# Attention followed by a squared-ReLU feed-forward: loads of later batches held back, batch 1's inputs loaded ahead of the weights, its turns moved into batch 0

## The chip, the cores and the metric

One core of a Trainium2 chip. The metric is device time in microseconds (us), lower is better. All runs quoted here were classed fast.

Names used for the engines in the profile: PE is TensorE (matrix multiplication; PEld its weight loads), ACT is ScalarE, DVE is VectorE, POOL is GpSimd, SP is the sync engine, which only issues transfers here.

Words used below: a **turn** is a transpose; on TensorE it is three matmuls against the identity matrix, and another engine copies its result out. **Idle matmuls** work on zeros, only to keep TensorE busy. The **granted clock** is the share of full speed that TensorE was given (1.00 is full); in a window it is a mean. A load **lands** when the last of its sixteen semaphore increments has come.

## The reference

```python
B, Hq, Hkv, S, D = 8, 16, 4, 384, 64                      # grouped-query attention, f32 inputs
scores = (q @ k.T) / sqrt(D)                              # k and v repeated 4 times over the heads
attn   = softmax(scores)                                  # per head, over 384 keys
x      = (attn @ v).transpose(0, 2, 1, 3).reshape(3072, 1024)
h      = maximum(x @ w_in, 0)                             # w_in 1024 x 2048
out    = (h * h) @ w_out                                  # w_out 2048 x 1024
```

## The kernel before

Eight batches (b0 to b7) of eight head pairs each. Pair n belongs to batch n // 8. The feed-forward network (FFN) of batch b runs on TensorE in between the attention of later batches. All inputs are f32 in HBM; loads issued by GpSimd cast them to bf16 on the way. Only b0 comes in as f32, over the queues of SP and ACT.

A recorder derives the semaphore waits; every engine runs its instructions in the order in which they are added. So an instruction that waits for data stops everything behind it on its engine. The order in which loads are added to GpSimd is also the order in which they get the DMA engines.

The loads and the start of b0 (cuts marked `...`):

```python
    cast_q(0)                       # f32 -> bf16 on GpSimd, one head pair
    load_w_in(0)                    # GpSimd queue, 0.52 MB of bf16 each
    cast_q(1)
    ...                             # v of b0
    for c in range(2, NPB):
        cast_q(c)
        load_w_in(c - 1)
    load_w_in(7)
    load_k(1); load_q(1); load_v(1) # one line each in the kernel
    for i in range(2):
        load_w_out(i)               # 2.10 MB of bf16 each
    load_k(2); load_q(2); load_v(2)
```

`prepare(b)`, called in pair 4 of the batch before, duplicates k of batch b on VectorE, turns k and q by DMA transposes on the sync queue, and then lets the loads of batch b + 1 go:

```python
    def prepare(b):
        dup_all_k(b)                # VectorE: waits for the load of k
        ...                         # dma_start_transpose of kT, then of qT in two parts
        if b + 1 < B:
            load_k(b + 1, [last])   # last = the second qT transpose
            load_q(b + 1, [last])
            load_v(b + 1, [last])
```

The main loop from pair 8 on. `fill(ns)` puts so much FFN work there; `put_x` turns a pair's attention output into x transposed (xT), by DMA. FFN(1) may start after pair 16, and needs xT of pair 15:

```python
    PER_PAIR = {1: 2700.0, **{b: 5100.0 for b in range(2, B + 1)}}
    ...
    for n in range(NPB, NP + 1):
        per = PER_PAIR[n // NPB]
        if n < NP:
            scores_pair(n)
        fill(per * 0.4)
        if n > NPB:
            attend(n - 1, 0)
        fill(per * 0.2)
        if n > NPB:
            attend(n - 1, 1)
            put_x(n - 1)
        if n % NPB == 4 and n // NPB + 1 < B:
            prepare(n // NPB + 1)
        if n % NPB == 7 and n // NPB + 1 < B:
            prepare_v(n // NPB + 1)
        fill(per * 0.4)
        ready[0] = max(0, n // NPB - 1)
```

The softmax here doesn't subtract the row's maximum and nothing guards it: scores larger than these inputs give would overflow.

Of the kernel before, what the change touches and what calls it, by code (L numbers as in the profile page):

```python
# [106 lines left out]
def bass_gqa_attention__then__ffn_squared_relu_kernel(  # L107
# [8 lines left out]
    bf16 = mybir.dt.bfloat16  # L116
    f32 = mybir.dt.float32

    B, H, S, D = 8, 16, 384, 64
    HKV = 4  # L120
    NJ = S // 128
    FF = 2048
    F = H * D
    NPB = H // 2
# [5 lines left out]
    R = Recorder(nc)  # L130
# [95 lines left out]
    for i in range(2):  # L226
        R.add("gpsimd", lambda e, i=i: e.memset(v_aug[i][:, :, D:D + 1], 1.0), writes=[("v_one", i)])

    def cast_q(c):
        R.add("gpsimd", lambda g: g.tensor_copy(q_st[0][:, 2 * c:2 * c + 2, :], q_f[:, 2 * c:2 * c + 2, :]),  # L230
              reads=[("q_f", c)], writes=[("q_st", 0, c)])

    cast_q(0)
    load_w_in(0)
    cast_q(1)
    R.add("gpsimd", lambda g: g.tensor_copy(
        v_aug[0][:, :, 0:D], v_f.ap().rearrange("p g j d -> p (g j) d")),
        reads=["v_f"], writes=[("v_aug", 0)])
    for c in range(2, NPB):
        cast_q(c)  # L240
        load_w_in(c - 1)
    load_w_in(7)
    load_k(1)
    load_q(1)
    load_v(1)
    for i in range(2):
        load_w_out(i)
    load_k(2)
# [19 lines left out]


    slots = [0]  # L270
    RING, FREE = (4, 5), (0, 1, 2, 3)
    sc_bf = sc_ps.ap().bitcast(bf16)

    def turn_bank(banks):
        i = banks[slots[0] % len(banks)]
        slots[0] += 1
        if i == 5:
            return f_ps[1].ap().bitcast(bf16)[:, 0:S], ("f_ps", 1)
        return sc_bf[:, i, 0:S], ("sc", i)

    def turn_on_pe(src, src_keys, dst, dst_key, banks):
        ps, key = turn_bank(banks)

        def tr(pe):
            for t in range(NJ):
                m = pe.matmul(ps[:, t * 128:(t + 1) * 128], src[:, t * 128:(t + 1) * 128], ident[:],  # L286
                              is_transpose=True)
            return m

        R.add("tensor", tr, reads=[*src_keys, "ident"], writes=[key])  # L290
        R.add("vector", lambda e: e.tensor_copy(dst, ps), reads=[key], writes=[dst_key])  # L291

    def dup_k(b, g):
        src = (k_f if b == 0 else k_st[b % NKS])[:, g].unsqueeze(2).to_broadcast([128, NJ, 2, D])
        R.add("vector", lambda e: e.tensor_copy(k_dup[b % 2][:, g * NJ:(g + 1) * NJ], src),
              reads=[("k_f", g) if b == 0 else ("k_st", b % NKS)], writes=[("k_dup", b % 2, g)])

    def first_kT(g, b=0):
        if b == 0:
            dup_k(0, g)  # L300
        turn_on_pe(k_dup[b][:, g * NJ:(g + 1) * NJ].rearrange("p a x d -> p (a x d)"), [("k_dup", b, g)],
                   kT[b][:, g], ("kT", b, g), FREE if b else RING)

    def first_qT(c, b=0):
        turn_on_pe(q_st[b][:, 2 * c:2 * c + 2, :].rearrange("p h e -> p (h e)"), [("q_st", b, c)],
                   qT[b][:, c], ("qT", b, c), FREE if b else RING)

    def first_oT(c, banks=RING):
        turn_on_pe(o_sb[c % NO].ap().rearrange("p i s d -> p (i s d)"), [("o_sb", c % NO, x) for x in range(2)],
                   xT[0][:, c], ("xT", 0, c), banks)  # L310

    def dup_all_k(b):
        src = k_st[b % NKS].ap().rearrange("p g j d -> p (g j) d").unsqueeze(2)
        R.add("vector", lambda e: e.tensor_copy(
            k_dup[b % 2][:, :, :, :], src.to_broadcast([128, HKV * NJ, 2, D])),
            reads=[("k_st", b % NKS)], writes=[("k_dup", b % 2, g) for g in range(HKV)])

    def prepare(b):
        st = b % NST
        dup_all_k(b)  # L320
        R.add("sync", lambda e: e.dma_start_transpose(
            kT[b % 2].ap().rearrange("p g (j c) -> p (g j) c", j=NJ),
            k_dup[b % 2].ap().rearrange("p a x d -> p (a x d)")),
            reads=[("k_dup", b % 2, g) for g in range(HKV)],
            writes=[("kT", b % 2, g) for g in range(HKV)], dma=f"kt{b % 2}")
        for part in range(2):
            cs = range(4 * part, 4 * part + 4)
            last = R.add("sync", lambda e, cs=cs: e.dma_start_transpose(
                qT[b % 2][:, cs.start:cs.stop, :].rearrange("p h (t c) -> p (h t) c", t=NJ),
                q_st[st][:, 2 * cs.start:2 * cs.stop, :].rearrange("p h e -> p (h e)")),  # L330
                reads=[("q_st", st, c) for c in cs], writes=[("qT", b % 2, c) for c in cs],
                dma=f"qt{b % 2}_{part}")
        if b + 1 < B:
            load_k(b + 1, [last])
            load_q(b + 1, [last])
            load_v(b + 1, [last])

    def prepare_v(b):
        R.add("vector", lambda e: e.tensor_copy(
# [73 lines left out]

    def put_x(p):
        b, c = p // NPB, p % NPB
        R.add("sync", lambda e: e.dma_start_transpose(
            xT[b % NXT][:, c, :].rearrange("p (i c) -> p i c", i=NJ),
            o_sb[p % NO].ap().rearrange("p i s d -> p (i s d)")),
            reads=[("o_sb", p % NO, x) for x in range(2)], writes=[("xT", b % NXT, c)], dma=f"xt{p % 8}")
# [2 lines left out]
    tiles = [0]  # L422

    def up_step(b, c, k0, k1, u, r):
        def mm(pe):
            for kc in range(k0, k1):
                m = pe.matmul(f_ps[u][:, 0:S], w_in_sb[:, kc, c * 128:(c + 1) * 128],  # L427
                              xT[b % NXT][:, kc, :], start=(kc == 0), stop=(kc == NKC - 1))
            return m

        R.add("tensor", mm, reads=[("w_in", c * 128 // WC)] +
              [("xT", b % NXT, kc) for kc in range(k0, k1)], writes=[("f_ps", u)])
        if k1 == NKC:
            R.add("vector", lambda e: e.tensor_scalar_max(hr[r][:, :], f_ps[u][:, 0:S], 0.0),  # L434
                  reads=[("f_ps", u)], writes=[("hr", r)])
            R.add("scalar", lambda e: e.activation(h2T[b % 2][:, c, :], hr[r][:, :], AF.Square),  # L436
                  reads=[("hr", r)], writes=[("h2T", b % 2, c)])
        return (k1 - k0) * 165
# [22 lines left out]
    def feed_forward(b):  # L461
        first = 0
        if b == 0:
            for c, k in ((0, 0), (0, 2), (0, 4), (1, 0), (1, 2), (1, 4), (0, 6), (1, 6)):
                yield up_step(b, c, k, k + 2, c, c)
            tiles[0] += 2
            first = 2
        for c in range(first, NFC):
            for k in range(0, NKC, 4):
                yield up_step(b, c, k, k + 4, tiles[0] % 2, tiles[0] % NHR)  # L470
            tiles[0] += 1
        for jj in range(2):
            for i in range(NJ):
                for part in range(4):
                    yield down_step(b, i, jj, part, tiles[0] % 2)
                tiles[0] += 1
# [9 lines left out]

    ffn = all_feed_forward()
    credit = [0.0]
    PER_PAIR = {1: 2700.0, **{b: 5100.0 for b in range(2, B + 1)}}

    def fill(ns):
        credit[0] += ns
        while credit[0] > 0:
# [3 lines left out]
                return  # L497
            credit[0] -= t

    idle(13)  # L500
    first_kT(0)
    idle(2)
    first_qT(0)
    idle(3)
    for n in range(NPB):
        early = n in (5, 6)
        scores_unit(n, 0)
        if early:
            next(ffn)
        elif n < 2:  # L510
            idle(2 - n)
        if n >= 1:
            attend(n - 1, 0)
        scores_unit(n, 1)
        if n % 2 == 1 and n + 1 < NPB:
            first_kT((n + 1) // 2)
        if n + 1 < NPB:
            first_qT(n + 1)
        if n >= 1:
            attend(n - 1, 1)  # L520
        scores_unit(n, 2)
        idle(1)
        if n >= 2:
            first_oT(n - 2)
    next(ffn)
    attend(NPB - 1, 0, True)
    first_oT(NPB - 2, (4,))
    attend(NPB - 1, 1, True)
    for _ in range(3):
        next(ffn)  # L530
    idle_on_sc(2)
    first_oT(NPB - 1, (0,))
    idle_on_sc(3)
    fill(6000.0)
    dup_all_k(1)
    fill(1500.0)
    for g in range(HKV):
        first_kT(g, 1)
        fill(700.0)
    prepare_v(1)  # L540
    for c in range(NPB):
        first_qT(c, 1)
        fill(500.0)
    for n in range(NPB, NP + 1):
        per = PER_PAIR[n // NPB]
        if n < NP:
# [4 lines that stand above are left out]
        fill(per * 0.2)  # L551
        if n > NPB:
            attend(n - 1, 1)
            put_x(n - 1)
        if n % NPB == 4 and n // NPB + 1 < B:
            prepare(n // NPB + 1)
        if n % NPB == 7 and n // NPB + 1 < B:
# [3 lines that stand above are left out]
# [32 lines left out]
```

## Time and profile before

447.52 us, median of 3 runs (445.23 to 447.89). What matters, from the profile of one execution (span 445.5 us):

| | before |
|---|---|
| TensorE busy | 430.6 us, 97% |
| first scores of b0 | 6.5 us |
| first scores of b1 (pair 8) | 47.9 us |
| wait for xT of pair 15 | 5.4 us idle, then low clock |
| granted clock 85 to 90, 90 to 95 us | 0.79, 0.53 |
| last landing of w_in, w_out; of k, q, v of b2 | 32.1, 58.4; 59.5, 64.5, 67.1 us |

The page of the kernel before: its first line, the busy times, and the granted clock in 40 slices of 11 us each (9 is full speed).

```profile
span 445.5 us, 8213 instructions
...
PE 430.6 (97%) x3589; PEld 239.8 (54%) x3626; DVE 165.9 (37%) x357; ACT 199.5 (45%) x209; POOL 33.2 (7%) x48
...
PEclk9999999979999999999999999999999999999999
```

The waits of TensorE in the kernel before, the longest in total: who waited for whom, total us, how often, the longest.

```profile
PE f_ps L427 <- DMA xT<-o_sb: 5.4, 1, 5.4
PE f_ps L256 <- DVE warm L221: 1.1, 1, 1.1
PE po L398 <- ACT expT L360: 0.9, 3, 0.4
```

The chain of waits of the kernel before, around the end of pair 16: start, us, what.

```profile
83.27 0.80 PE f_ps L445 x3
84.07 6.76 DMA xT<-o_sb
90.82 0.05 issue
90.87 4.00 PE f_ps L427 x12
```

The same stretch in windows: start and end, length, then busy us of PE, PEld, DVE, ACT, POOL, and last the granted clock, the DMA share and GB/s.

```profile
80.00:85.00 5.00, 4.95 (x45) 2.57 (x45) 1.63 (x4) 2.37 (x2) 0.00 (x0) 1.00 1.16 130
85.00:90.00 5.00, 0.43 (x3) 0.04 (x1) 0.00 (x0) 1.81 (x1) 0.00 (x0) 0.79 1.49 180
90.00:95.00 5.00, 4.13 (x22) 2.12 (x23) 0.65 (x2) 0.52 (x1) 0.00 (x0) 0.53 0.13 39
```

And the transfers issued from 76 to 90 us: KB each, median us from issue to landing.

```profile
q_st<-in_q_dram POOLq DMA_DIRECT2D x1, 768.0 KB, 12.5
...
xT<-o_sb SPq DMA_TRANSPOSE x3, 6.8
```

Read together: TensorE is the limit nearly everywhere, and its one large idle stretch is a wait for a small transfer that shares the DMA engines with a load nobody needs yet. Over the whole trace such a transfer takes 2.4 us (median). The rules table of the Trainium skill's page "DMA: Bandwidth & Descriptors" (section "Rules for kernel authors") says that queues of different engines run on the same 16 DMA engines and interleave; the 6.8 us here, on the sync queue beside a GpSimd load, agree.

### The profile page before, as it was taken

The page shows a single profiled execution, that of the slowest core. Times are in us where ns is not written, and L with a number is a line of the kernel's source. Part 1 is how long each engine was busy: PE and PEld are TensorE (multiplying, and loading weights), DVE is VectorE, ACT ScalarE, POOL GpSimd, SP SyncE. Part 2 cuts the span into 40 slices and gives each one's busy share as a digit, 9 for nine tenths or more (in the row PEclk, how much of TensorE's full clock was granted, in tenths as well). Part 3 has the DMA queues.
Part 4 walks back from the last instruction along what each step waited for, and adds up shares of the span by engine and source line. Part 5 has one row for each costly group of instructions (what it writes and reads, how often), then busy time and mean ns, then how long its engine had stood idle before and what let it go on. Part 6 is the DMA issues. An engine that isn't in the chain of part 4 may idle for free.

```text
span 445.5 us, 8213 instructions
## 1 busy us (share of the span) xinstructions
PE 430.6 (97%) x3589; PEld 239.8 (54%) x3626; DVE 165.9 (37%) x357; ACT 199.5 (45%) x209; POOL 33.2 (7%) x48
## 2 busy tenths in 40 slices
PE   8989999689999999999999999999999999999997
PEld 4556555346545665456644565456655565545543
DVE  2646432224423442334423434234423344224411
ACT  4953655325533564336632565236633466203400
POOL 5920001000020001000020000100000000000000
PEclk9999999979999999999999999999999999999999
DMA  9999998920495108920399106951252200220011
GB/s 244 197 196 203 209 192 190 147 43 16 90 167 122 43 10 149 175 85 10 76 147 151 45 20 126 139 113 42 32 135 82 66 20 18 66 81 24 1 71 71
DMA packets 95939, 44.70 MB, mean 100 GB/s; under 512 B 74400, under 2 KB 89760, under 8 KB 95904
## 3 DMA queue, kind: packets, MB, share of 16 engines
q0 software_dynamic: 34288, 16.65, 30.0%
q1 hardware_dynamic: 59504, 25.96, 25.4%
q10 hardware_dynamic: 2112, 1.57, 1.1%
q8 instruction: 28, 0.46, 0.5%
q14 instruction: 7, 0.06, 0.0%
HBM read 35.65 MB, written 12.58 MB: 108 GB/s over the span
## 4 chain that ended last, share of the span: by engine, by line
PE 94%; DMA 2%; DVE 2%; ACT 1%; issue 1%
PE f_ps L427 38%; PE f_ps L445 37%; PE po L398 8%; PE sc_ps L370 7%; DMA xT<-o_sb 2%; PE sc_ps L354 1%; ACT expT L360 1%; PE sc_ps L286 1%; DMA k_f<-in_k_dram 1%; PE f_ps L256 1%; DVE o_sb L411 0%; DVE qT L291 0%; DVE xT L291 0%; PE f_ps L286 0%; DVE hr L434 0%
## 5 line engine op out<-in xcount | busy, mean ns | idle before, releaser
L427 PE MATMUL f_ps<-xT,w_in_sb 128*128 128x384 bf16 x1024 | 184.7, 329 | 6.6 <-DMA xT<-o_sb 5.4
L445 PE MATMUL f_ps<-w_out_sb,h2T 128*128 128x512 bf16 x731 | 176.4, 379 | 2.2 <-issue 0.5
L387 ACT ACTIVATE expT<-sc_ps 128x2304 bf16<-128x2304 f32 x56 | 116.8, 2086 | 100.5 <-PE sc_ps L370 98.8
L427 PEld LDWEIGHTS f_ps<-xT,w_in_sb 128*128 128x128 bf16 x1024 | 93.7, 98 | 69.6 <-issue 7.8
L436 ACT ACTIVATE h2T<-hr 128x384 bf16<-128x384 f32 x128 | 66.7, 521 | 115.0 <-DVE hr L434 113.5
L434 DVE TENSOR_SCALAR hr<-f_ps 128x384 f32<-128x384 f32 x128 | 71.1, 556 | 107.5 <-PE f_ps L427 107.5
L445 PEld LDWEIGHTS f_ps<-w_out_sb,h2T 128*128 128x128 bf16 x768 | 68.7, 97 | 75.7 <-issue 5.9
L454 DVE COPY y_sb<-f_ps 128x512 f32<-128x512 f32 x48 | 33.2, 691 | 101.4 <-PE f_ps L445 98.4
L398 PEld LDWEIGHTS po<-v_aug,expT 128*128 128x128 bf16 x1143 | 51.7, 98 | 23.6 <-ACT expT L360 2.5
L398 PE MATMUL po<-v_aug,expT 128*128 128x65 bf16 x1143 | 56.3, 194 | 1.2 <-ACT expT L360 0.9
L370 PE MATMUL sc_ps<-qT,kT 64*128 64x128 bf16 (+2 forms) x504 | 37.2, 272 | 0.2 <-DVE qT L291 0.2
L411 DVE TENSOR_TENSOR o_sb<-po,rinv 128x384 bf16<-128x384 f32 x64 | 35.5, 555 | 2.2
L370 PEld LDWEIGHTS sc_ps<-qT,kT 64*128 64x128 bf16 x504 | 20.6, 94 | 22.1 <-issue 17.1
L408 DVE RECIPROCAL rinv<-po 128x6 f32<-128x6 f32 x64 | 12.3, 192 | 51.2 <-PE po L398 51.2
L167 POOL DMA_DIRECT2D k_st<-in_k_dram x7 | 5.3, 760 | 242.3 <-DMA qT<-q_st 242.3
L360 ACT ACTIVATE expT<-sc_ps 128x768 bf16<-128x768 f32 x24 | 18.6, 809 | 5.0 <-PE sc_ps L354 4.2
L256 PE MATMUL f_ps<-warm 128*128 128x256 bf16 x29 | 7.7, 379 | 1.5 <-DVE warm L221 1.1
L354 PE MATMUL sc_ps<-qT,kT 64*128 64x384 bf16 x48 | 8.7, 358 | 0.0
L181 POOL DMA_DIRECT2D q_st<-in_q_dram x7 | 8.3, 1179 | 0.0
L189 POOL DMA_DIRECT2D w_in_sb<-in_moe_w_in_dram x8 | 7.1, 893 | 0.0
L256 PEld LDWEIGHTS f_ps<-warm 128*128 128x128 bf16 x29 | 3.3, 125 | 4.7 <-DVE qT L291 1.5
L291 DVE COPY qT<-sc_ps 128x384 bf16<-128x384 bf16 x12 | 4.0, 350 | 4.1 <-PE sc_ps L286 4.1
(40 smaller groups left out, 54.0 us busy)
## 6 DMA issues: line engine op xcount, KB each, us to landing
out_dram<-y_sb SPq DMA_DIRECT2D x48, 256.0 KB, 2.3
q_st<-in_q_dram POOLq DMA_DIRECT2D x7, 768.0 KB, 12.5
w_in_sb<-in_moe_w_in_dram POOLq DMA_DIRECT2D x8, 512.0 KB, 10.6
w_out_sb<-in_moe_w_out_dram POOLq DMA_DIRECT2D x2, 2048.0 KB, 33.3
k_st<-in_k_dram POOLq DMA_DIRECT2D x7, 192.0 KB, 5.0
v_st<-in_v_dram POOLq DMA_DIRECT2D x7, 192.0 KB, 13.1
xT<-o_sb SPq DMA_TRANSPOSE x56, 2.4
q_f<-in_q_dram ACTq DMA_DIRECT2D x1, 768.0 KB, 8.5
```

Of the source, the lines that this page charges most:

```text
L256: m = pe.matmul(f_ps[1][:, 0:256], warm[:, 0:128], warm[:, 0:256])
L354: m = pe.matmul(sc_ps[:, 2 * u + x, 0:S], kt[rows, j * 128:(j + 1) * 128], qt[rows, :])
L360: R.add("scalar", lambda e: e.activation(dst, src, AF.Exp, scale=0.125), reads=[("sc", 2 * u), ("sc", 2 * u + 1)], writes=[("expT", p % NE ...
L370: return pe.matmul(sc_flat[:, at + c0:at + c1], kt[rows, j * 128:(j + 1) * 128], qt[rows, c0:c1])
L387: R.add("scalar", lambda e: e.activation(dst, src, AF.Exp, scale=0.125), reads=sc_keys, writes=[("expT", p % NEX, j) for j in range(NJ)])
L398: m = pe.matmul(acc[:, i, s, :], expT[p % NEX][:, j, f * 128:(f + 1) * 128], v_aug[b % 2][:, g * NJ + j, :], start=(j == 0), stop=(j == NJ ...
L411: R.add("vector", lambda e: e.tensor_tensor(o_sb[p % NO][:, :, ss, :], acc[:, :, ss, 0:D], rb, ALU.mult), reads=[acc_key, ("rinv", p % 2)] ...
L427: m = pe.matmul(f_ps[u][:, 0:S], w_in_sb[:, kc, c * 128:(c + 1) * 128], xT[b % NXT][:, kc, :], start=(kc == 0), stop=(kc == NKC - 1))
L434: R.add("vector", lambda e: e.tensor_scalar_max(hr[r][:, :], f_ps[u][:, 0:S], 0.0), reads=[("f_ps", u)], writes=[("hr", r)])
L436: R.add("scalar", lambda e: e.activation(h2T[b % 2][:, c, :], hr[r][:, :], AF.Square), reads=[("hr", r)], writes=[("h2T", b % 2, c)])
L445: m = pe.matmul(f_ps[u][:, :], h2T[b % 2][:, c, i * 128:(i + 1) * 128], w_out_sb[:, c, jj * 512:(jj + 1) * 512], start=(c == 0), stop=(c = ...
L454: R.add("vector", lambda e: e.tensor_copy(y_sb[yb][:, :], f_ps[u][:, :]), reads=[("f_ps", u)], writes=[("y", yb)])
```

## The change: intent and diff

Four things, cut to their core:

```diff
-    cast_q(0)
-    load_w_in(0)
+    dup_k(0, "vector")                      # k copies of b0: pair 0 on VectorE, the others on GpSimd
+    cast_q(0, "vector")
     cast_q(1)
     ...                                     # v of b0
+    dup_k(1, "gpsimd")
+    load_q(1)                               # b1 ahead of w_in
+    cast_q(2)
+    load_k(1)
+    cast_q(3)
+    load_w_in(0)
+    ...                                     # casts, dup_k(2), dup_k(3), load_w_in(1..3) in turn
     load_v(1)
+    for i in range(4, NWB):
+        load_w_in(i)
     for i in range(2):
         load_w_out(i)
     load_k(2)                               # q2, v2 behind it, as before
@@ prepare(b)
-        if b + 1 < B:
-            load_k(b + 1, [last]); load_q(b + 1, [last]); load_v(b + 1, [last])
@@ b0: seven of the twelve turns of b1's k and q stand in pairs 4 to 7
+        if n >= 4:
+            turns.pop(0)()                  # a turn on TensorE, a copy on VectorE
+        if n == 3:
+            dup_all_k(1)                    # VectorE: waits for the load of k1
+        if n in (4, 6, 7):
+            turns.pop(0)()
     ...                                     # 3 + 5 + 4 FFN steps on three accumulators, no idle matmuls
-    PER_PAIR = {1: 2700.0, ...
+    PER_PAIR = {1: 3700.0, ...
@@ main loop
-            put_x(n - 1)
+            landed = put_x(n - 1)
+            if n % NPB == 1 and 2 * NPB < n < (B - 1) * NPB:
+                for load in (load_k, load_q, load_v):
+                    load(n // NPB + 1, [landed])
```

The intent: pair 15's transfer travels alone; gaps of TensorE in b0 do work of b1; more of FFN(0) lies behind b1's attention, so that something covers that transfer.

More of the change, by code (lines that the diff above doesn't have):

```diff
@@ L227, in bass_gqa_attention__then__ffn_squared_relu_kernel, with cast_q, dup_k @@
         R.add("gpsimd", lambda e, i=i: e.memset(v_aug[i][:, :, D:D + 1], 1.0), writes=[("v_one", i)])
-    def cast_q(c):
-        R.add("gpsimd", lambda g: g.tensor_copy(q_st[0][:, 2 * c:2 * c + 2, :], q_f[:, 2 * c:2 * c + 2, :]),
+    def cast_q(c, eng="gpsimd"):
+        R.add(eng, lambda g: g.tensor_copy(q_st[0][:, 2 * c:2 * c + 2, :], q_f[:, 2 * c:2 * c + 2, :]),
               reads=[("q_f", c)], writes=[("q_st", 0, c)])
-    cast_q(0)
-    load_w_in(0)
+    def dup_k(g, eng):
+        src = k_f[:, g].unsqueeze(2).to_broadcast([128, NJ, 2, D])
+        R.add(eng, lambda e: e.tensor_copy(k_dup[0][:, g * NJ:(g + 1) * NJ], src),
+              reads=[("k_f", g)], writes=[("k_dup", 0, g)])
+    dup_k(0, "vector")
+    cast_q(0, "vector")
     cast_q(1)
@@ L238, in bass_gqa_attention__then__ffn_squared_relu_kernel @@
         reads=["v_f"], writes=[("v_aug", 0)])
-    for c in range(2, NPB):
-        cast_q(c)
-        load_w_in(c - 1)
-    load_w_in(7)
+    dup_k(1, "gpsimd")
+    load_q(1)
+    cast_q(2)
     load_k(1)
-    load_q(1)
+    cast_q(3)
+    load_w_in(0)
+    cast_q(4)
+    dup_k(2, "gpsimd")
+    load_w_in(1)
+    cast_q(5)
+    load_w_in(2)
+    cast_q(6)
+    dup_k(3, "gpsimd")
+    load_w_in(3)
+    cast_q(7)
     load_v(1)
+    for i in range(4, NWB):
+        load_w_in(i)
     for i in range(2):
@@ L270, in bass_gqa_attention__then__ffn_squared_relu_kernel @@
     slots = [0]
-    RING, FREE = (4, 5), (0, 1, 2, 3)
+    RING, FREE = (4, 5, 6), (0, 1, 2, 3)
     sc_bf = sc_ps.ap().bitcast(bf16)
@@ L276, in turn_bank, with turn_on_pe @@
         slots[0] += 1
-        if i == 5:
-            return f_ps[1].ap().bitcast(bf16)[:, 0:S], ("f_ps", 1)
+        if i >= 5:
+            return f_ps[i - 5].ap().bitcast(bf16)[:, 0:S], ("f_ps", i - 5)
         return sc_bf[:, i, 0:S], ("sc", i)
-    def turn_on_pe(src, src_keys, dst, dst_key, banks):
+    def turn_on_pe(src, src_keys, dst, dst_key, banks, eng="vector"):
         ps, key = turn_bank(banks)
@@ L290, in turn_on_pe, with first_kT, first_qT, first_oT @@
         R.add("tensor", tr, reads=[*src_keys, "ident"], writes=[key])
-        R.add("vector", lambda e: e.tensor_copy(dst, ps), reads=[key], writes=[dst_key])
-    def dup_k(b, g):
-        src = (k_f if b == 0 else k_st[b % NKS])[:, g].unsqueeze(2).to_broadcast([128, NJ, 2, D])
-        R.add("vector", lambda e: e.tensor_copy(k_dup[b % 2][:, g * NJ:(g + 1) * NJ], src),
-              reads=[("k_f", g) if b == 0 else ("k_st", b % NKS)], writes=[("k_dup", b % 2, g)])
-    def first_kT(g, b=0):
-        if b == 0:
-            dup_k(0, g)
+        if eng == "scalar":
+            R.add(eng, lambda e: e.copy(dst, ps), reads=[key], writes=[dst_key])
+        else:
+            R.add(eng, lambda e: e.tensor_copy(dst, ps), reads=[key], writes=[dst_key])
+    def first_kT(g, b=0, banks=RING):
         turn_on_pe(k_dup[b][:, g * NJ:(g + 1) * NJ].rearrange("p a x d -> p (a x d)"), [("k_dup", b, g)],
-                   kT[b][:, g], ("kT", b, g), FREE if b else RING)
-    def first_qT(c, b=0):
+                   kT[b][:, g], ("kT", b, g), banks)
+    def first_qT(c, b=0, banks=RING):
         turn_on_pe(q_st[b][:, 2 * c:2 * c + 2, :].rearrange("p h e -> p (h e)"), [("q_st", b, c)],
-                   qT[b][:, c], ("qT", b, c), FREE if b else RING)
-    def first_oT(c, banks=RING):
+                   qT[b][:, c], ("qT", b, c), banks)
+    def first_oT(c, banks=RING, eng="vector"):
         turn_on_pe(o_sb[c % NO].ap().rearrange("p i s d -> p (i s d)"), [("o_sb", c % NO, x) for x in range(2)],
-                   xT[0][:, c], ("xT", 0, c), banks)
-    def dup_all_k(b):
+                   xT[0][:, c], ("xT", 0, c), banks, eng)
+    def dup_all_k(b, eng="vector"):
         src = k_st[b % NKS].ap().rearrange("p g j d -> p (g j) d").unsqueeze(2)
-        R.add("vector", lambda e: e.tensor_copy(
+        R.add(eng, lambda e: e.tensor_copy(
             k_dup[b % 2][:, :, :, :], src.to_broadcast([128, HKV * NJ, 2, D])),
@@ L327, in prepare @@
             cs = range(4 * part, 4 * part + 4)
-            last = R.add("sync", lambda e, cs=cs: e.dma_start_transpose(
+            R.add("sync", lambda e, cs=cs: e.dma_start_transpose(
                 qT[b % 2][:, cs.start:cs.stop, :].rearrange("p h (t c) -> p (h t) c", t=NJ),
@@ L332, in prepare @@
                 dma=f"qt{b % 2}_{part}")
-        if b + 1 < B:
-            load_k(b + 1, [last])
-            load_q(b + 1, [last])
-            load_v(b + 1, [last])
     def prepare_v(b):
@@ L415, in put_x @@
         b, c = p // NPB, p % NPB
-        R.add("sync", lambda e: e.dma_start_transpose(
+        return R.add("sync", lambda e: e.dma_start_transpose(
             xT[b % NXT][:, c, :].rearrange("p (i c) -> p i c", i=NJ),
@@ L424, in up_step @@
     def up_step(b, c, k0, k1, u, r):
+        acc, key = (f_ps[u].ap(), ("f_ps", u)) if u < 2 else (sc_ps[:, 2], ("sc", 2))
         def mm(pe):
             for kc in range(k0, k1):
-                m = pe.matmul(f_ps[u][:, 0:S], w_in_sb[:, kc, c * 128:(c + 1) * 128],
+                m = pe.matmul(acc[:, 0:S], w_in_sb[:, kc, c * 128:(c + 1) * 128],
                               xT[b % NXT][:, kc, :], start=(kc == 0), stop=(kc == NKC - 1))
@@ L431, in up_step @@
         R.add("tensor", mm, reads=[("w_in", c * 128 // WC)] +
-              [("xT", b % NXT, kc) for kc in range(k0, k1)], writes=[("f_ps", u)])
+              [("xT", b % NXT, kc) for kc in range(k0, k1)], writes=[key])
         if k1 == NKC:
-            R.add("vector", lambda e: e.tensor_scalar_max(hr[r][:, :], f_ps[u][:, 0:S], 0.0),
-                  reads=[("f_ps", u)], writes=[("hr", r)])
+            R.add("vector", lambda e: e.tensor_scalar_max(hr[r][:, :], acc[:, 0:S], 0.0),
+                  reads=[key], writes=[("hr", r)])
             R.add("scalar", lambda e: e.activation(h2T[b % 2][:, c, :], hr[r][:, :], AF.Square),
@@ L463, in feed_forward @@
         if b == 0:
-            for c, k in ((0, 0), (0, 2), (0, 4), (1, 0), (1, 2), (1, 4), (0, 6), (1, 6)):
+            for c, k in [(c, k) for c in range(3) for k in (0, 2, 4)] + [(c, 6) for c in range(3)]:
                 yield up_step(b, c, k, k + 2, c, c)
-            tiles[0] += 2
-            first = 2
+            first = 3
         for c in range(first, NFC):
@@ L488, in bass_gqa_attention__then__ffn_squared_relu_kernel @@
     credit = [0.0]
-    PER_PAIR = {1: 2700.0, **{b: 5100.0 for b in range(2, B + 1)}}
+    PER_PAIR = {1: 3700.0, **{b: 5100.0 for b in range(2, B + 1)}}
     def fill(ns):
@@ L498, in fill @@
             credit[0] -= t
+    turns = [lambda banks=RING, g=g: first_kT(g, 1, banks) for g in range(HKV)]
+    turns += [lambda banks=RING, c=c: first_qT(c, 1, banks) for c in range(NPB)]
     idle(13)
-    first_kT(0)
-    idle(2)
-    first_qT(0)
-    idle(3)
+    first_kT(0, banks=(4,))
+    idle(1)
+    first_qT(0, banks=(6,))
     for n in range(NPB):
-        early = n in (5, 6)
+        ring = (4, 6) if n < 4 else RING
         scores_unit(n, 0)
-        if early:
-            next(ffn)
-        elif n < 2:
-            idle(2 - n)
+        if n >= 4:
+            turns.pop(0)()
+        else:
+            idle(2 if n == 0 else 1)
         if n >= 1:
@@ L515, in bass_gqa_attention__then__ffn_squared_relu_kernel @@
         if n % 2 == 1 and n + 1 < NPB:
-            first_kT((n + 1) // 2)
+            first_kT((n + 1) // 2, banks=ring)
         if n + 1 < NPB:
-            first_qT(n + 1)
+            first_qT(n + 1, banks=ring)
+        if n == 3:
+            dup_all_k(1)
         if n >= 1:
@@ L521, in bass_gqa_attention__then__ffn_squared_relu_kernel @@
         scores_unit(n, 2)
-        idle(1)
+        if n < 4:
+            idle(1)
         if n >= 2:
-            first_oT(n - 2)
-    next(ffn)
-    attend(NPB - 1, 0, True)
-    first_oT(NPB - 2, (4,))
-    attend(NPB - 1, 1, True)
+            first_oT(n - 2, ring)
+        if n in (4, 6, 7):
+            turns.pop(0)()
     for _ in range(3):
         next(ffn)
-    idle_on_sc(2)
-    first_oT(NPB - 1, (0,))
-    idle_on_sc(3)
-    fill(6000.0)
-    dup_all_k(1)
-    fill(1500.0)
-    for g in range(HKV):
-        first_kT(g, 1)
-        fill(700.0)
+    attend(NPB - 1, 0, True)
+    first_oT(NPB - 2, (4,), "scalar")
+    attend(NPB - 1, 1, True)
+    for _ in range(5):
+        next(ffn)
+    first_oT(NPB - 1, (0,))
+    for _ in range(4):
+        next(ffn)
     prepare_v(1)
-    for c in range(NPB):
-        first_qT(c, 1)
-        fill(500.0)
+    while turns:
+        turns.pop(0)(FREE)
+        fill(600.0)
     for n in range(NPB, NP + 1):
```

## The prediction

> **What bounds it now.** The page: TensorE busy 430.6 of 445.5 us (97%), 94% of the chain of waits. Only its gaps, waits and low clock can be won. Warm durations from the chain (up matmul 0.163 us, down 0.216, batch-0 scores 0.137, turn 0.167, attend of nine 0.283, scores pair 0.60) put the necessary work at about 414 us; some 32 us are overhead. In the chain in order of time:
>
> 1. To the first scores: 6.6 us.
> 2. Batch 0's attention, 6.6 to 27.7 us. ScalarE sets the pace: 24 exps of 0.815 us = 19.6; TensorE has gaps.
> 3. 27.7 to 31.9 us: waits for exp, xT and hr, and idle matmuls: about 1.4 us beyond the work.
> 4. 84.07 to 90.87 us: TensorE waits for the transfer xT<-o_sb of batch 1's last output. It took 6.8 us against a median of 2.4: the loads of b3 (issued 75.95 to 78.6, landed by about 90.4) share the DMA engines. The next 12 matmuls take 4.00 us instead of 1.95, at a granted clock of 0.53. The Trainium skill, "TensorE: Matmul & The Clock Gate", Part 1, says so of idle windows (half clock after about 3.4 us); the trace agrees. Sum: 8.85 us.
>
> From 95 us on TensorE is continuously busy; only the 3 us tail is left, and stays.
>
> **What the change does.**
> - Loads of b3 and later wait for the first transposed output of the batch after; pair 15's xT travels alone. FFN(0) is stretched (3.7 us per pair of batch 1 instead of 2.7), leaving about 5 us for pair 16, so the 2.4 us transfer and 0.75 us normalisation are nearly covered. I expect 0.3 to 1.5 us of stall and no fall of the clock: -8 us.
> - Seven of b1's twelve turns (1.2 us) move into gaps of b0; three early FFN steps (1.0 us) leave those gaps but cover the last exp: -1 us.
> - Third accumulator, xT copy on ScalarE, no idle matmuls at the end: -1.2 us.
> - k copies and the first q cast change engines: first scores near 5.6 us. But VectorE now copies all of k1 (0.55 us) in pair 3. q1 and k1 (0.98 MB at the traced 0.197 MB/us, from about 10 us, plus 0.9 us to the semaphore) land near 16 us, when VectorE wants them at about 15.5; most of the lead is lost again. Net -0.3 us.
> - w_in lands 5 to 6 us later (last near 38 us), but its use is spread out later still; w_out lands as before (48, 58 us), needed from 54. No stall. k2 may hold VectorE 1 to 3 us near 60 us; two accumulators cover that.
>
> GpSimd's added copies cost about 0.5 us each (its same-size casts take 0.51); it has slack.
>
> **Time.** -10.5 us: **437.0 us**, range 433 to 441.5. Faster by over 2%: 0.76, within 2%: 0.23, slower: 0.01.
>
> **What would show it.** No wait for xT<-o_sb over 1.5 us; clock 1.0 after 10 us; b1's first scores near 36 us (before 47.9); last exp of b0 near 27 us; w_in never a releaser; span about 435.
>
> **What would make it wrong.** VectorE, at about 2.2 us of work per 2.45 us pair in pairs 4 to 7, stalls the exps; k1 comes later than 16 us; transposes of pairs 12 to 15 queue behind b2's q transposes, which wait for q2, so that batch 2's scores or FFN(1) stall; later loads collide with a transfer then needed.

## The result, and the profile after

441.64 us median of 4 runs (441.39 to 441.91), against 446.57 us (4 runs of before). The ratio is 0.989 (95% interval 0.9853 to 0.9927). Later (after_again below) the same kernel gave 440.81 us, ratio 0.9871 (0.9846 to 0.9895). A ratio is the mean time of one kernel's fast runs over that of the other's of the same rounds, so not quite the ratio of the medians quoted. The change is real, about 1.1 to 1.3%, and about half of what was predicted.

The page and TensorE's waits of the changed kernel. L302 is a turn, L326 is the copy of all of k1, L272 an idle matmul.

```profile
span 439.3 us, 8230 instructions
...
PE 431.0 (98%) x3615; PEld 239.4 (55%) x3615; DVE 164.8 (38%) x354; ACT 199.5 (45%) x210; POOL 34.1 (8%) x50
```

```profile
PE f_ps L302 <- DVE k_dup L326: 2.5, 1, 2.5
PE f_ps L272 <- DVE warm L221: 1.1, 1, 1.1
```

The wait for xT is gone from the list. The chain of waits of the changed kernel at that place:

```profile
83.58 0.57 DVE o_sb L419
84.15 0.02 issue
84.17 2.29 DMA xT<-o_sb
86.46 0.05 issue
86.51 1.47 PE f_ps L437 x8
```

The transfer takes 2.29 us instead of 6.76, and TensorE has other work meanwhile: it is busy throughout, at full clock (windows of the changed kernel):

```profile
80.00:85.00 5.00, 5.00 (x41) 2.45 (x41) 1.45 (x3) 1.32 (x1) 0.00 (x0) 1.00 0.23 75
85.00:90.00 5.00, 4.88 (x50) 2.99 (x50) 1.92 (x4) 3.07 (x3) 0.00 (x0) 1.00 0.22 72
```

But there is a new wait, at the top of the list: 2.5 us in b0. The chain of waits there:

```profile
9.62 8.58 DMA k_st<-in_k_dram
18.20 0.02 issue
18.22 0.77 DVE k_dup L326
19.00 0.11 DVE rinv L416
19.11 0.02 issue
19.13 0.57 DVE o_sb L419
19.70 0.14 issue
19.83 0.63 PE po L406 x9
```

And the windows of the changed kernel around it:

```profile
10.00:15.00 5.00, 4.75 (x66) 2.89 (x64) 2.58 (x8) 4.56 (x7) 5.00 (x9) 1.00 1.40 156
15.00:20.00 5.00, 2.06 (x30) 1.33 (x29) 2.36 (x7) 2.27 (x3) 5.00 (x8) 0.99 1.49 197
20.00:25.00 5.00, 5.00 (x64) 3.37 (x61) 2.78 (x9) 3.12 (x4) 5.00 (x6) 0.67 1.45 197
```

VectorE's waits for k in the changed kernel (two: k1 2.4 us, k2 0.6 us):

```profile
DVE k_dup L326 <- DMA k_st<-in_k_dram: 3.0, 2, 2.4
```

The load of k1 lands at 18.2 us. VectorE stands at `dup_all_k(1)` for 2.4 us, so it turns no bank free and normalises nothing; TensorE is busy for only 2.06 us of 5; ScalarE waits 3.5 us in one piece for its next scores; and after the pause TensorE runs at a mean granted clock of 0.67 in the next window: the clock was at half from 19.9 to 23.3 us. The last exp of b0 ends at 30.9 us, where 27 was predicted.

To see where time is won and lost I use one more quantity. **TensorE overhead at pair n** is the start of pair n's first scores matmul in the trace, less the TensorE work that stands ahead of it in program order, at warm durations read from the trace (up matmul 0.163 us, down 0.216, turn 0.167, attend of nine 0.282, scores of b0 0.137 per matmul, a later scores pair 0.62; idle matmuls count as nothing). Where it stays level, TensorE does useful work at full speed; where it jumps, time was lost. It creeps up by about 0.08 us per pair in all kernels. It scatters from one execution to the next: kernels in which b0, and the order of the loads that it meets, are the same differ there by 0.7 us (before and e5; after, after_again and e4) and by 1.2 us (e1, e8, e9, e10 and e12), so smaller differences at pair 8 show nothing. One profile each (after_again is the changed kernel, later):

| kernel | pair 8 | 14 | 16 | 17 | 18 | 63 |
|---|---|---|---|---|---|---|
| before | 15.2 | 15.7 | 15.9 | 16.0 | 23.5 | 27.2 |
| after | 16.2 | 16.7 | 16.8 | 16.9 | 17.3 | 20.9 |
| after_again | 15.5 | 16.0 | 16.2 | 16.3 | 16.6 | 20.3 |

From pair 17 to 18 the kernel before loses 7.5 us and the changed one 0.4: the change wins 7.1 us there. Up to pair 8 it loses 1.0 us instead of winning 2.5 (0.3 in the second profile). The sum, 6.1 to 6.3, is the difference of the spans (445.5 - 439.3 = 6.2 us). So the question is what became of the start.

### The profile page after: what moved, and what is told of

Its sections match the earlier page's. It is cut to its first block, busy times and chain, and to the rows that moved or that the text cites. A ratio compares the mean times of both kernels' runs of the same rounds, so it can differ in the third digit from the quotient of the medians.

```text
span 439.3 us, 8230 instructions
## 1 busy us (share of the span) xinstructions
PE 431.0 (98%) x3615; PEld 239.4 (55%) x3615; DVE 164.8 (38%) x354; ACT 199.5 (45%) x210; POOL 34.1 (8%) x50
## 4 chain that ended last, share of the span: by engine, by line
PE 93%; DMA 4%; DVE 1%; POOL 1%; issue 0%; ACTq 0%
PE f_ps L437 38%; PE f_ps L455 38%; PE po L406 8%; PE sc_ps L378 7%; DMA k_st<-in_k_dram 2%; DMA q_f<-in_q_dram 1%; PE sc_ps L362 1%; DMA xT<-o_sb 1%; PE f_ps L302 0%; PE sc_ps L302 0%; DVE o_sb L419 0%; POOL q_st L181 0%; PE sc_ps L437 0%; POOL q_st L230 0%; DVE k_dup L326 0%
## 5 line engine op out<-in xcount | busy, mean ns | idle before, releaser
L437 PE MATMUL f_ps<-xT,w_in_sb 128*128 128x384 bf16 x1016 | 181.4, 326 | 0.2
L455 PE MATMUL f_ps<-w_out_sb,h2T 128*128 128x512 bf16 x768 | 180.3, 379 | 0.0
L437 PEld LDWEIGHTS f_ps<-xT,w_in_sb 128*128 128x128 bf16 x1016 | 92.4, 97 | 61.4 <-issue 6.3
L444 DVE TENSOR_SCALAR hr<-f_ps 128x384 f32<-128x384 f32 x127 | 70.6, 556 | 99.9 <-PE f_ps L437 99.9
L406 PE MATMUL po<-v_aug,expT 128*128 128x65 bf16 x1143 | 57.3, 195 | 0.8 <-DVE o_sb L419 0.4
L378 PEld LDWEIGHTS sc_ps<-qT,kT 64*128 64x128 bf16 x504 | 20.6, 94 | 21.7 <-issue 16.1
L416 DVE RECIPROCAL rinv<-po 128x6 f32<-128x6 f32 x64 | 12.3, 192 | 43.7 <-PE po L406 43.6
L368 ACT ACTIVATE expT<-sc_ps 128x768 bf16<-128x768 f32 x24 | 18.8, 809 | 8.0 <-PE sc_ps L362 7.5
L272 PE MATMUL f_ps<-warm 128*128 128x256 bf16 x23 | 6.2, 387 | 1.1 <-DVE warm L221 1.1
L174 POOL DMA_DIRECT2D v_st<-in_v_dram x7 | 5.5, 781 | 0.0
L326 DVE COPY k_dup<-k_st 128x1536 bf16<-128x1536 bf16 x7 | 4.1, 583 | 3.0 <-DMA k_st<-in_k_dram 3.0
## 6 DMA issues: line engine op xcount, KB each, us to landing
w_in_sb<-in_moe_w_in_dram POOLq DMA_DIRECT2D x8, 512.0 KB, 13.9
v_st<-in_v_dram POOLq DMA_DIRECT2D x7, 192.0 KB, 10.4
```

The source lines that it names most:

```text
L368: R.add("scalar", lambda e: e.activation(dst, src, AF.Exp, scale=0.125), reads=[("sc", 2 * u), ("sc", 2 * u + 1)], writes=[("expT", p % NE ...
L378: return pe.matmul(sc_flat[:, at + c0:at + c1], kt[rows, j * 128:(j + 1) * 128], qt[rows, c0:c1])
L406: m = pe.matmul(acc[:, i, s, :], expT[p % NEX][:, j, f * 128:(f + 1) * 128], v_aug[b % 2][:, g * NJ + j, :], start=(j == 0), stop=(j == NJ ...
L416: R.add("vector", lambda e: e.reciprocal(rinv_v, acc[:, :, ss, D:D + 1]), reads=[acc_key], writes=[("rinv", p % 2)])
L437: m = pe.matmul(acc[:, 0:S], w_in_sb[:, kc, c * 128:(c + 1) * 128], xT[b % NXT][:, kc, :], start=(kc == 0), stop=(kc == NKC - 1))
L444: R.add("vector", lambda e: e.tensor_scalar_max(hr[r][:, :], acc[:, 0:S], 0.0), reads=[key], writes=[("hr", r)])
```

## The experiments

Theory A: the late load of k1 is what the start lost. Rival B: pairs 4 to 7 are overfull with the seven extra turns and their copies, as the prediction feared. The overhead of all kernels is in one table at the end of this section.

### e1: k1 loaded before q1

```diff
-    load_q(1)
+    load_k(1)
     cast_q(2)
-    load_k(1)
+    load_q(1)
```

> Changed kernel with one edit: the load of k1 is issued before that of q1. Theory A (the late k1 load holds VectorE in pair 3, which holds TensorE 2.5 us and ScalarE 3.5 us and drops the clock): k1 lands near 13 us, VectorE waits for no load in pair 3, last exp of b0 ends near 27 us instead of 30.9, b1's first scores near 36 instead of 39.8, time about 437.8 us. Rival B (VectorE or TensorE is overfull in pairs 4 to 7 because of the seven extra turns): the hold goes but the exps stall in pairs 4 to 7, b1's first scores stay at 38 us or later, time 440 us or more.

Measured: 440.38 us (438.64 to 441.59), ratio 0.9856 (0.9818 to 0.9895). k1 landed near 12 us, b1's first scores began at 35.1 us, and the overhead at pair 8 was 11.6 us: 4.6 less than in the changed kernel. So much for rival B: with k1 in time, pairs 4 to 7 hold all seven turns. But the median fell by about 1 us only, between different calls and with overlapping intervals, so a faster time is not shown. VectorE's longest waits for a transfer in e1, and the windows of e1 after it, say why:

```profile
DVE k_dup L326 <- DMA k_st<-in_k_dram: 7.7, 1, 7.7
```

```profile
60.00:65.00 5.00, 5.00 (x51) 2.54 (x47) 0.00 (x0) 2.09 (x1) 0.00 (x0) 1.00 1.91 211
65.00:70.00 5.00, 2.91 (x30) 1.53 (x29) 2.72 (x7) 2.09 (x1) 0.00 (x0) 0.95 1.34 157
70.00:75.00 5.00, 5.00 (x24) 1.82 (x22) 0.46 (x1) 1.34 (x1) 0.00 (x0) 0.71 1.24 194
```

Everything runs 4.6 us earlier, but the load of k2 does not: it lands at 67 us, and VectorE, already at pair 12's `dup_all_k(2)`, does nothing from 59.2 to 67.0. TensorE runs out of free accumulators and stands about 2 us, then runs at a clock of 0.71. The overhead goes from 12.1 at pair 14 to 15.9 at pair 15: 3.8 of the 4.6 us are given back. Theory A was right about the start and wrong about the time. This calls for a third theory.

### e2: k1 still later

```diff
-    load_k(1)
     cast_q(3)
     load_w_in(0)
+    load_k(1)
```

> Changed kernel with the load of k1 issued one w_in piece later (0.52 MB at 0.197 MB/us more in front of it). Theory A: k1 lands about 2.7 us later, near 21 us, VectorE is held about 5 us instead of 2.4, and the time grows by about the same, to 444.3 us (443.3 to 445.5). Rival B: under 1 us of change.

Measured: 444.21 us (443.2 to 444.73), ratio 0.9949 (0.9913 to 0.9985), which overlaps the interval of the change's first call and not that of its second. VectorE was held 4.2 us and TensorE 4.4, the overhead at pair 8 was 17.9, against 15.5 to 16.2 in the three profiles with the change's own order. The dose acts as expected in both directions: the load order of 0.2 MB decides the start.

### e3: TensorE kept busy during the hold

```diff
+        if n == 4:
+            ...                             # 21 idle matmuls on accumulator f_ps[0]
         if n >= 4:
             turns.pop(0)()
```

> Changed kernel with 21 idle matmuls (about 2.3 us) on a free accumulator ahead of the turn that waits for k1's copies, so that TensorE does not fall idle during the hold; the late load itself stays. Splits the loss into wait and low clock. Theory A: VectorE is held as long as before, but the clock stays at 1.0 in 20 to 25 us and about 1 to 1.5 us come back: 440.4 us. If the low clock costs nothing because ScalarE sets the pace, 441.6 us.

Measured: 440.07 us (438.98 to 440.85), ratio 0.9851 (0.9817 to 0.9885), near the 440.4 expected. The clock stayed at 1.00 in the windows from 10 to 45 us. But the test is not clean: in the profiled execution k1 landed 1.6 us sooner, at 16.6, and held VectorE for 1.3 us only, and the interval overlaps that of the changed kernel. That the low clock has a cost of its own is likely; its size stays open.

### e4: the loads of b3 and on where they were

```diff
+        if b + 1 < B:                       # in prepare(b), as before
+            load_k(b + 1, [last]); load_q(b + 1, [last]); load_v(b + 1, [last])
-            landed = put_x(n - 1)           # and no loads in the main loop
+            put_x(n - 1)
```

> Changed kernel with the loads of b3 and on put back where the kernel before had them (after b2's q transposes). If the deferral is what removed the 6.8 us transfer of pair 15: the transfer takes 5 us or more again, TensorE waits at the end of pair 16, the clock falls, time 446 to 449 us. Rival (the 5 us of FFN(0) kept for pair 16 alone were enough): under 443 us.

Measured: 448.62 us (447.73 to 449.38), ratio 1.0043 (1.001 to 1.0076): slower than the kernel before. The chain of waits of e4:

```profile
83.75 7.44 DMA xT<-o_sb
91.20 0.05 issue
91.24 2.74 PE f_ps L441 x8
```

The transfer of pair 15 is back at 7.44 us, and the overhead jumps by 7.0 from pair 17 to 18. The 5 us of FFN(0) kept for pair 16 do not help without the deferral.

### e5: the deferral alone, in the kernel before

```diff
     # on the kernel before
-        if b + 1 < B: ...                   # loads in prepare(b)
+            landed = put_x(n - 1)           # loads in the main loop, as in the change
```

> The kernel before with one part of the change alone: loads of b3 and on wait for the first transposed output of the batch after. Theory A: pair 15's transfer falls to about 2.4 us, TensorE waits about 1.2 us for it instead of 5.4 (only 2 us of other work lie behind it at 2.7 us per pair), the clock stays up, -6.3 us: 440.2 us (439 to 441.5), as fast as the whole change. Rival (the deferral needs the stretched FFN(0) to be worth anything): 444 us or more.

Measured: 440.06 us (439.7 to 440.31), ratio 0.9854 (0.9832 to 0.9876). One part of the change alone is as fast as the whole of it, as far as these runs can tell (the two did not run in the same rounds, and their intervals overlap). TensorE waits 1.0 us for pair 15's transfer, and the clock is 1.0. The three other parts together bring no time that these runs show; locally the stretched FFN(0) is worth 0.8 us, since the overhead grows by 1.2 us from pair 17 to 18 here and by 0.4 in the whole change.

### e8: k1 and k2 both early

Theory C: by the end of b1 the loads fill the DMA engines, so a faster b0 only meets the next late load.

```diff
     # and e1's edit
-    for i in range(2):
-        load_w_out(i)
-    load_k(2)
+    load_w_out(0)
+    load_k(2)
+    load_w_out(1)
     load_q(2)
```

> Changed kernel with k1 loaded before q1 and k2 loaded between the two halves of w_out. In the run with k1 first, b1 began at 35 us and then VectorE was held 7.7 us for k2, which cost 3.8 us in pair 14. Theory A': this second late load is where that gain went; k2 lands near 52 us, VectorE waits for no load after pair 0, no wait of TensorE over 1 us in pairs 8 to 17, time about 436.7 us (435.5 to 438). Rival (the gain is lost to something else in b1, such as DMA traffic of w_out and transposes): 439.5 us or more.

Measured: 441.73 us (441.21 to 442.27), ratio 0.9893 (0.9872 to 0.9914). The expectation failed. VectorE no longer waits for k2, which landed at 54 us. TensorE's waits in e8:

```profile
PE sc_ps L378 <- issue: 3.2, 1, 3.2
PE f_ps L437 <- DMA xT<-o_sb: 1.9, 1, 1.9
```

The first is batch 2's first scores. The profile finds no releaser for it, but the order of events does: q2 landed at 73.7 us, its two transposes were issued from 73.73 us on, the scores began at 77.54. The sync queue had waited 9.1 us for q2, and the transposes of pairs 12 to 15 stood behind it, which is the second wait. So with k1 and k2 in time it is q2 that is late. That is what theory C says, though I had expected only one more late load.

### e6: all twelve turns after b0

```diff
     # on e8: no turns in pairs 4 to 7
-        if n >= 4:
-            turns.pop(0)()
-        if n in (4, 6, 7):
-            turns.pop(0)()
```

> As the run with k1 and k2 early, but all twelve turns of b1 after b0, as the kernel before had them. If the gaps of b0 were free (theory A), moving seven turns back costs their own time, 7 x 0.167 = 1.2 us: 437.9 us. If the seven turns and their copies hold up the exps (rival B), the time stays or falls: 436.7 us or less.

Measured: 440.57 us (439.82 to 440.94), ratio 0.9864 (0.9841 to 0.9888). The overhead at pair 8 is 13.3 against 12.0 in e8, and against 11.6 to 12.8 in all five kernels with e8's start. The direction is that of turns which are free in the gaps, and the size fits their own 1.2 us, but with this scatter the size is not shown. The total, however, is not slower than e8: q2 landed at 70.6 us here, 3.1 us sooner than in e8, and the overhead grew by 2.3 us from pair 14 to 18 instead of 5.7. Why q2 came sooner is not shown. By the time alone rival B would have been believed; the overhead at pair 8, here and in e1, speaks against it.

### e7: the k copies of b0 back on VectorE

```diff
     # on e8
-    dup_k(1, "gpsimd") ... dup_k(2, "gpsimd") ... dup_k(3, "gpsimd")
+            dup_k((n + 1) // 2, "vector")   # ahead of each turn of k in b0
```

> As the run with k1 and k2 early, but the three later k copies of b0 on VectorE as before instead of GpSimd. VectorE then has 2.8 to 2.9 us of work in pairs 3 and 5 against a pace of 2.45: the exps should stall about 0.5 us in each of the two, time +0.5 to +1.2 us: 437.5 us. If the engine of these copies does not matter: 436.7 us.

Measured: 440.54 us (439.92 to 442.65), ratio 0.9861 (0.9838 to 0.9884). The overhead at pair 8 is 12.5, half a us above e8, which is inside the scatter; the time is again not slower. The run is inconclusive, about the start and about the time.

### e9: half of w_out not loaded (wrong result)

```diff
     # and e1's edit
-    for i in range(2):
-        load_w_out(i)
+    load_w_out(0)
+    memset of the other half of w_out_sb to 0.01 on GpSimd
```

> Result wrong on purpose: changed kernel with k1 first, and the second half of w_out is filled by GpSimd with a constant instead of loaded, which takes 2.1 MB (10.7 us at 0.197 MB/us) out of the queue of loads ahead of k2, q2 and v2. Theory C (the loads needed by the end of b1 fill the DMA engines, so a faster b0 only meets the next late load: k2 in one run, q2 in the next): q2 lands near 63 us instead of 74, TensorE has no wait over 1 us in pairs 8 to 17, overhead stays near 12.7 us up to pair 17, time about 436.4 us (435 to 437.8). Rival (b1 itself, its transposes on the sync queue or its order, sets the pace): 439.5 us or more.

Measured: 436.98 us (436.54 to 437.22), ratio 0.979 (0.9762 to 0.9818). q2 landed at 57.4 us (earlier than expected), the overhead stays between 11.6 and 12.3 up to pair 17, and TensorE's longest waits are:

```profile
PE f_ps L272 <- DVE warm L221: 1.0, 1, 1.0
PE po L406 <- ACT expT L368: 0.7, 2, 0.4
PE f_ps L455 <- issue: 0.6, 4, 0.2
```

Nothing in b1 itself sets the pace. With 2.1 MB taken out of the queue of loads, the rest of the change's gain appears, and the time is the 437.0 us predicted for the change. That the two agree so well is partly luck: the start won 3.6 us where 2.5 was predicted, and all that follows 7.3 where 8 was. The waits that went are the verdict for theory C.

The mean DMA rate over the first 70 us says the same. One line of windows each, of before, of after, of e1 and of e8; the last number is GB/s:

```profile
0.00:70.00 70.00, 65.59 (x641) 38.71 (x645) 32.55 (x86) 39.98 (x47) 19.97 (x33) 1.00 1.27 204
```
```profile
0.00:70.00 70.00, 64.98 (x634) 38.32 (x635) 31.38 (x83) 40.85 (x49) 20.80 (x35) 0.98 1.31 200
```
```profile
0.00:70.00 70.00, 64.69 (x657) 38.56 (x661) 31.71 (x86) 42.47 (x49) 21.17 (x35) 1.00 1.32 197
```
```profile
0.00:70.00 70.00, 66.46 (x675) 39.31 (x675) 32.10 (x86) 42.36 (x49) 21.24 (x35) 1.00 1.29 195
```

None of these orders of the loads moves more: 195 to 204 GB/s in all four. An estimate from the traced sizes: w_in and w_out 8.39 MB, all of b1 1.18, k2 and q2 0.98 are 10.55 MB of bf16, which at 0.197 MB/us and from about 10 us on is done at 63.5 us, without any transpose or output store in between. In the kernel before, q2 landed at 64.5 us, long before b2's first scores at 79.3 us. In e8 b2's first scores could have started at 74.

### e10 and e12: four outputs of b1 turned on TensorE

The DMA transposes of b1's outputs run beside the w_out load. In the changed kernel those issued from 45 to 62 us took 7.7 us (median) and take DMA time from the loads. Both runs build on e8.

```diff
+    # pairs 8 to 11: turn on TensorE into the other FFN accumulator, copy on VectorE
+        if NPB <= n - 2 <= 11:
+            turn_x(n - 2)                   # e12: in the middle of the next FFN tile instead
-            landed = put_x(n - 1)
+            if n - 1 > 11:
+                landed = put_x(n - 1)
```

> Right result: changed kernel with k1 before q1 and k2 between the halves of w_out, and the outputs of pairs 8 to 11 turned on TensorE (0.167 us each, 0.7 us in all, copies on VectorE) instead of by DMA transposes, which ran beside the w_out load and took 8 us each. Theory C: about 2 us of DMA time per transpose comes free, q2 lands near 66 to 68 us instead of 74, batch 2's first scores no longer wait 3.2 us and pair 15's transfer not 1.9; time about 437.7 us (436.5 to 439). Rival: 440 us or more.

Measured: 439.62 us (438.62 to 440.15), ratio 0.9848 (0.9821 to 0.9874). q2 landed at 66.9 us instead of 73.7, and both waits of e8 are gone: from pair 14 to 18 the overhead grows by 0.7 only (e8: 5.7). New waits took part of it back: TensorE waited 0.9 us for the new copies, and the overhead grew by 1.5 us from pair 10 to 12; the start was 0.8 us worse than e8's in this execution, which is inside the scatter.

> Right result: as the run with four outputs of b1 turned on TensorE, but each turn is put in the middle of a feed-forward tile instead of where it fell. In that run two turns stood at a tile's end, and the next tile waited for their copy (TensorE waits for the xT copies, 0.9 us; overhead grew by 1.6 us from pair 10 to 12). Expected: overhead grows by under 0.6 us there, no wait for q2, k2 or pair 15's transfer over 0.5 us, time about 438.3 us (437.3 to 439.3), faster than the change (440.8) and than the other run (439.6). If the tile order did not matter: 439.6 us.

Measured: 439.22 us (438.65 to 440.73), ratio 0.9849 (0.9821 to 0.9878). The overhead grew by 0.7 us from pair 10 to 12 instead of 1.5, but one copy is still waited for (0.6 us). The time can't be told from e10's.

The changed kernel, again, on e10's chip:

> The changed kernel itself, on the same chip as these runs: 441.6 us as before, with k1 landing near 18 us and TensorE held about 2.5 us in pair 4.

Measured: 440.81 us (439.22 to 440.95). VectorE was held 1.2 us for k1, which landed at 18.7, and TensorE waited 1.5 us for it, less than the 2.5 expected. The clock fell in this execution too, but before that wait, as its windows show: it was at half from 12.6 to 16.0 us, after TensorE had waited 1.1 us for a cast of q on GpSimd (to 10.4 us).

```profile
10.00:15.00 5.00, 4.42 (x49) 2.66 (x49) 2.15 (x6) 2.87 (x4) 5.00 (x9) 0.76 1.19 137
15.00:20.00 5.00, 3.47 (x41) 2.12 (x40) 2.26 (x6) 3.40 (x5) 5.00 (x8) 0.90 1.50 196
```

e10 and e12 have the lowest medians of the kernels with a right result, some 7 us below before. Against the changed kernel e10 is ahead by 1.2 us in the same rounds, 439.62 to 440.81, with overlapping intervals, so it is not shown to be faster than the change or than e5.

All overheads (us, one profile each) and medians:

| kernel | pair 8 | 14 | 16 | 17 | 18 | 63 | median us |
|---|---|---|---|---|---|---|---|
| e1 k1 first | 11.6 | 12.1 | 16.0 | 16.1 | 16.4 | 20.1 | 440.38 |
| e2 k1 later | 17.9 | 18.4 | 18.5 | 18.6 | 19.0 | 22.6 | 444.21 |
| e3 idle matmuls | 13.7 | 14.2 | 14.4 | 14.4 | 14.8 | 18.4 | 440.07 |
| e4 loads early | 15.8 | 16.3 | 16.4 | 16.5 | 23.5 | 27.2 | 448.62 |
| e5 before, deferral | 14.5 | 15.0 | 15.2 | 15.3 | 16.5 | 20.1 | 440.06 |
| e8 k1, k2 early | 12.0 | 12.4 | 15.9 | 15.9 | 18.1 | 21.7 | 441.73 |
| e6 e8, no gap turns | 13.3 | 13.8 | 13.9 | 14.8 | 16.1 | 19.8 | 440.57 |
| e7 e8, k on VectorE | 12.5 | 13.0 | 15.0 | 15.1 | 18.8 | 22.5 | 440.54 |
| e9 less to load | 11.6 | 12.0 | 12.2 | 12.3 | 12.7 | 16.3 | 436.98 |
| e10 turns of x | 12.8 | 14.5 | 14.7 | 14.8 | 15.2 | 18.8 | 439.62 |
| e12 the same, mid-tile | 12.7 | 13.6 | 13.8 | 13.9 | 14.3 | 17.9 | 439.22 |

(e7's profile fell on its slowest run, 442.65 us.)

## Why the prediction was right or wrong

The prediction was 437.0 us (433 to 441.5); 441.64 was measured, and 440.81 later. About half of the gain came. Step by step:

**Right: the stall of pair 15.** Predicted "-8 us"; the overhead shows 7.1. The mechanism held in both directions (e4, e5). The size was a little high because "Sum: 8.85 us" counted the whole 6.8 us as lost, though about 1.2 us of it were batch 2's second scores pair (0.60) and four matmuls (0.65) that were due anyway.

**Right: the clock.** That it would not fall after pair 16 held. That it would be "1.0 after 10 us" failed: in the first profile after the pause for k1, in after_again already after the wait for a cast of q. The Trainium skill's "TensorE: Matmul & The Clock Gate", Part 1, was cited for the half clock after idle time; the changed kernel shows half clock after idle time again, a mean of 0.67 in 20 to 25 us, but the pause for k1 was only 2.5 us long.

**Right: the gaps of b0.** Seven turns fit with no cost that shows (e1, e6), and the end of b0 without idle matmuls too: with k1 in time, b1's first scores began at 35.1 us (e1; 36 was predicted) and the overhead at pair 8 fell by 3.6 us against before.

**Wrong: "q1 and k1 ... land near 16 us, when VectorE wants them at about 15.5; most of the lead is lost again. Net -0.3 us."** This is the step that failed, in its landing time and in its cost; the prediction had named "k1 comes later than 16 us" as a risk. k1 landed at 18.2. Of the 2.2 us, about 1 is the rate: the queue wrote 156 GB/s in 10 to 15 us, not the 197 of the same window of the kernel before, where the loads were under way already. The rest is the semaphore. I took 0.9 us from the last bytes to it, but k1's sixteen increments came from 15.9 to 18.2 us in the trace: fourteen of them by 16.8, the last two at 17.3 and 18.2. The Trainium skill's "DMA: Bandwidth & Descriptors", section "Why a DMA increments its semaphore by 16 and not by 1", says that only the full 16 means that all data have landed; the trace agrees, and the slowest of the sixteen is what VectorE waits for. And the cost was mis-sized with it: an in-order VectorE held for 2.4 us stopped TensorE for 2.5 us, ScalarE for 3.5, and took the clock down, so that the start, predicted at -2.5 us, came out at +1.0 (+0.3 in the second profile). That is 3.5 of the 4.3 us missing between the predicted 10.5 and the 6.2 of the spans; the stall's size is the other 0.8.

**Named as a risk but not counted: what a good start would have met.** The prediction said of k2 "1 to 3 us near 60 us; two accumulators cover that", and listed among what could go wrong that pairs 12 to 15 might "queue behind b2's q transposes, which wait for q2"; neither stood in its sum. It also had w_out landing "as before (48, 58 us)". In the changed kernel it landed at 50.5 and 62.6, and k2 and q2 at 64.4 and 69.6, about 5 us later than before. From 45 to 62 us the GpSimd queue moved 3.09 MB instead of 3.30, and three transposes of b1's outputs were issued in that time instead of two, b1 having begun 8 us sooner. That is about 1 us of the 5; the slow beginning of the queue is another, and the rest is not traced. In the changed kernel the late k2 was harmless (0.6 us), but only because b0 was late. With the start repaired VectorE is held 7.7 us for k2 (e1), and with that repaired q2 is late (e8). The one run in which the predicted gain appears is e9, with a quarter of the weights' bytes not loaded. So where the expected gain of the start went is settled for these versions: into the wait for k1 in the change as it is, and into k2 and q2 as soon as that is mended.

**Open:** the cost of the low clock by itself (e3), which pauses bring it on, and why k1 lands between 16.6 and 18.7 us from one execution to the next.

## What to carry to other kernels

Before you make a stage faster, list all loads in their order of issue with the time at which each lands at the traced rate, counted to the slowest DMA engine, and set it beside the time at which the faster stage will need them: the first one that is late turns into the new limit, and an in-order engine that stands at it stops the others. Holding back a load that nobody needs yet cost nothing and won 6 us here by itself; moving one ahead delays all behind it. And judge a local edit by a local quantity, such as the overhead at a fixed point: e6 looked useful by the time alone, though its start was the later one. But measure first how much that local quantity scatters between executions; here it was up to 1.2 us.

## What the Trainium skill lacked or had wrong

- "DMA: Bandwidth & Descriptors", section "Bandwidth": it gives GB/s by transfer size, but not for loads that cast. Here f32 to bf16 loads wrote 197 GB/s (twice that read, by the sizes), in either order of k1 and q1, but less while the queue began: 156 from 10 to 15 us in the changed kernel, where q1 came first, and 141 in e1, where k1 did.
- The same page, section "Why a DMA increments its semaphore by 16 and not by 1": it doesn't say how far apart the sixteen come. Here they spread over 2.3 us for k1 (15.9 to 18.2 us), over 0.4 us for the same load in e1 (11.2 to 11.6 us), and over 4.3 us for the first half of w_out in e8 (48.7 to 53.0 us), for transfers of 0.2 and 2.1 MB.
- The same page, section "DMA Transpose (X-bar)": no figure for a transpose beside a load. Here 2.3 to 2.4 us alone; beside one, medians of 6.8 us (before, 76 to 90 us) and 7.7 us (after, 45 to 62 us).
- "TensorE: Matmul & The Clock Gate", Part 1: it puts the half clock after an idle window of about 3.4 us. Here less was enough: half clock came after a pause of 2.5 us, one turn and a further 0.44 us (after, 19.9 to 23.3 us), and after one pause of 1.9 us (e1, 69.5 to 72.9 us). A pause of 3.2 us (e8, up to 77.5 us) was followed by none. So the length of a pause alone did not tell.
